# Pooled attention and two feed-forward layers on one core: v in a buffer per head, preparation and weight conversions at other tiles, and layer 1's tanh in two tiles by turns

## The chip, the cores and the metric

One Trainium2 chip, of which one core is used. The metric is the device time of one execution in microseconds (us). Three runs of the kernel before give 1400.29, 1396.39 and 1401.53 us, with 1400.29 us as their median. A separate profiled execution, from which every row below comes, took 1398.61 us.

## What is computed

The reference, cut to what matters (B, H, S, D = 4, 8, 1152, 64):

```python
q_pool = q.reshape(B, H, S // 2, 2, D).mean(axis=3)
scores = (1 / sqrt(D)) * q_pool @ k.transpose(0, 1, 3, 2)
attn = exp(scores - max(scores)); attn = attn / (sum(attn) + 1e-9)
x = (attn @ v) laid out as 2304 tokens x 512
h = x @ w_in;  x = (h - tanh(h)) @ w_out            # layer 1, 512 -> 2048 -> 512
h = x @ w2_in; x = (h * sigmoid(1.702 h)) @ w2_out  # layer 2
```

The weights arrive as 64-bit floats, the rest as 32-bit floats.

## The kernel before

Everything is matrix products of float32 numbers split in a high and a low part, so that one product becomes three matmuls (high x high, high x low, low x high). The order of all instructions on every engine is written out by hand; each engine takes its own in order.

**Attention.** Heads are handled in 16 pairs. A pair has 18 steps (`NS`), nine key tiles of 128 for each of its two heads; the step within the pair is `i`, and the running step is `g`. In a step, `scores(g)` makes a tile of scores on TensorE (PE) in two halves and ScalarE (ACT) takes each half twice through the exponential (`pf` in float32, `ph` rounded); `rest(g-1)` subtracts the two on VectorE (DVE), or on GpSimd (POOL) at i = 2, 5, 8 and 11 of the tile's own step; `pv(g-3)` multiplies with v on PE. At every second step `max_tile` makes a block of scores for the *next* pair and DVE reduces it to row maxima (L284), in one PSUM tile, so the next block waits until the reduction of the last one is done.

The preparation of later pairs lies between: SyncE's queue (SP) loads q, k and v; `prep_qs`, `prep_qh`, `prep_ql`, `prep_kh`, `prep_kl`, `prep_bdq` split them; `stack` copies parts into the layout of the score matmuls (six SP transfers a head); `prep_v(p, s)` splits v of head s of pair p on POOL (L301 and L304). The table `plan` says at which step of a pair each is issued, for the pair two or three ahead. The buffer of v holds a whole pair and there is one: `load_v(p+2)` is issued at i = 14, after `prep_v(p+1, 1)` at i = 12, and `prep_v(p+2, 0)` wants it at i = 3 of the pair that follows.

**Weights of the first steps of layer 1.** The table `when` gives for each of eight pieces of weights (kind `i` for w_in, `o` for w_out) the pair and the step, counted from the end, of its load and of three conversion steps: s0 (one ACT, two DVE instructions, L122 to L127), s1 (two DVE, L134 and L138), and the split (one ACT, L145, one POOL, L146). There are two buffers for raw pieces. What has no step in the table (`ahead`) is done in the first steps of layer 1. `split_x` splits the first block of layer 1's input, one ACT and one POOL instruction for each of four columns.

**Layers.** Each layer is 48 steps `n` (four quarters of the 2048 columns, six blocks of 384 tokens, two halves). A step has 24 matmuls `h_part(n)` and 24 (layer 1) or 18 longer ones (layer 2) `y_part(n-2)` on PE, and `gate(n)` between them. In layer 1 the gate is a polynomial for small h and h - tanh(h) for others: ACT makes u = h*h (L586), d = tanh(h) (L587), later three more squares or cuts of u (L599, L601, L605); DVE makes five instructions (L588, L594, L603, L606, L608), the last of which copies d into g where |h| is large. Between them stand `split_g(n-1)` (ACT L562, POOL L564), which `y_part(n-1)` needs, the additions of y into x (`add`, on ACT in the first quarter, on DVE later) and the conversions of further weights. The tiles u, a, e and d are single, g is double, and h lies in two PSUM tiles.

Of the kernel before, what the change touches and what calls it, by code (L numbers as in the profile page):

```python
# [7 lines left out]
F32 = mybir.dt.float32  # L8
F32R = mybir.dt.float32r
I32 = mybir.dt.int32  # L10
AF = mybir.ActivationFunctionType
ALU = mybir.AluOpType
# [11 lines left out]
def f32(ap):  # L24
    return ap.bitcast(F32)
# [3 lines left out]
def tile_pooled_attention_two_moe(  # L29
# [11 lines left out]
    nc = tc.nc  # L41
    B, NPB, _, S = k.shape
    NT, DM = out.shape
    D = 64
    SP = S // 2
    HB = SP // 2
    KT = S // 128
    QJ = SP // 64
    NPAIR = B * NPB
    TB = 384  # L50
# [10 lines left out]
    wpool = ctx.enter_context(tc.tile_pool(name="wpool", bufs=1))  # L61
# [18 lines left out]
    def new(name, shape, dt=F32R):  # L80
        return wpool.tile(shape, dt, name=name)
# [6 lines left out]
    bdqs = [new(f"bdq{i}", [128, QJ, 128]) for i in range(2)]  # L88
# [9 lines left out]
    def split_x(b, cs, eng):  # L98
        for c in cs:
            hi, lo = xs[b][0][c], xs[b][1][c]  # L100
            nc.scalar.activation(hi, xb[b][:, c], AF.Copy)
            eng.tensor_tensor(lo, xb[b][:, c], f32(hi), op=ALU.subtract)
# [83 lines left out]
    def attention(ctx: ExitStack):  # L186
        ap = ctx.enter_context(tc.tile_pool(name="attn", bufs=1))
# [11 lines left out]
        def fill(i):  # L199
            vh, vl = vt[i]  # L200
            nc.gpsimd.memset(f32(stacks[i][1][D:D + 1, :]), 1.0)
            nc.gpsimd.memset(f32(vh[:, :, D:128]), 1.0)
            nc.gpsimd.memset(f32(vl[:, :, D:128]), 0.0)
# [7 lines left out]
        qraw, kraw, vraw, pairs = {}, {}, {}, {}  # L211
# [5 lines left out]
        def load_k(p):  # L217
            kraw[p] = ap.tile([128, S], F32, tag="kr", name="kr", bufs=2)
            nc.sync.dma_start(out=kraw[p], in_=k[p // NPB, p % NPB])

        def load_v(p):
            vraw[p] = ap.tile([128, 2, KT, D], F32, tag="vr", name="vr")
            nc.sync.dma_start(out=vraw[p], in_=v[p // NPB, p % NPB])

        def prep_qs(p, eng=None):
            pairs[p] = dict(
# [9 lines left out]
        def prep_qh(p):  # L236
            nc.scalar.activation(pairs[p]["qh"], pairs[p]["qs"], AF.Copy)
# [2 lines left out]
            d = pairs[p]  # L240
            nc.vector.tensor_sub(d["ql"], d["qs"], f32(d["qh"][:]))

        def prep_bdq(p):
            qs = pairs[p]["qs"]
            for s in range(2):
                r = slice(64 * s, 64 * s + 64)
                nc.scalar.activation(
                    bdqs[p % 2][r, :, r], qs[r, :].rearrange("p (j c) -> p j c", j=QJ), AF.Copy)

        def prep_kh(p, x):  # L250
            xs = slice(x * SP, (x + 1) * SP)
            nc.scalar.activation(pairs[p]["kh"][:, xs], kraw[p][:, xs], AF.Copy)
# [7 lines left out]
        def prep_kl(p, x):  # L260
            xs = slice(x * SP, (x + 1) * SP)
            nc.gpsimd.tensor_tensor(
                pairs[p]["kl"][:, xs], kraw[p][:, xs], f32(pairs[p]["kh"][:, xs]),
                op=ALU.subtract)
# [12 lines left out]
        def max_tile(p, j, pool=None):  # L277
            d = pairs[p]
            mx = (pool or ps_mx).tile([128, 3, 512], F32, tag="mx", name="mx")
            for a in range(3):  # L280
                nc.tensor.matmul(  # L281
                    mx[:, a, 0:384], bdqs[p % 2][:, j, :], d["kh"][:, a * 384:(a + 1) * 384],
                    start=True, stop=True)
            nc.vector.tensor_reduce(  # L284
                d["mt"][:, j:j + 1], mx[:, :, 0:384], AX.XY, ALU.max, negate=True)
# [10 lines left out]
                    queues[a].dma_start(out=row[:, :, a, :], in_=f32(tt[g:g + QJ, :]))  # L296

        def prep_v(p, s):
            vr = vraw[p]
            vh, vl = vt[(2 * p + s) % 3]  # L300
            nc.gpsimd.tensor_scalar(  # L301
                out=vh[:, :, 0:D], in0=vr[:, s], scalar1=1.0, scalar2=1.0,
                op0=ALU.mult, op1=ALU.mult)
            nc.gpsimd.tensor_tensor(  # L304
                vl[:, :, 0:D], vr[:, s], f32(vh[:, :, 0:D]), op=ALU.subtract)

        probs, accs, halves = {}, {}, {}

# [72 lines left out]

        def spread(p):
            d = norm[p]
            d["rb"] = wpool.tile([128, SP], F32, tag="rb", name="rb", bufs=1)
            for s in range(2):
                r = slice(64 * s, 64 * s + 64)
                row = d["rd"][r, :].rearrange("p i -> (p i)").unsqueeze(0)
                nc.sync.dma_start(out=d["rb"][r, :], in_=row.to_broadcast([64, SP]))

        def normalise(p):  # L390
            ua, rb = norm[p]["ua"], norm[p]["rb"]
# [12 lines left out]
        pool_cast = range(NPAIR * NS - NS + 2, NPAIR * NS, 3)  # L404
        early = {}
        when = (
# [8 lines left out]
        )  # L415
        ahead = []
        for kind, f, *steps in when:
# [3 lines left out]
            ahead += jobs[len(steps):]  # L421
        for c in range(NKC):
            early.setdefault((NPAIR - 1, 13 + c), []).append(
                lambda c=c: split_x(0, [c], nc.gpsimd))

        load_q(0)
        load_k(0)
# [6 lines left out]
            out=pairs[0]["kh"][:, SP:S], in0=kraw[0][:, SP:S],  # L434
            scalar1=1.0, scalar2=1.0, op0=ALU.mult, op1=ALU.mult)
        prep_qh(0)
        prep_ql(0)
        load_q(1)
        load_k(1)
        load_v(0)  # L440
        prep_kl(0, 0)
        prep_kl(0, 1)
        stack(0, 0)
# [3 lines left out]
        with tc.tile_pool(name="ps_first", bufs=2, space=PSUM) as ps_first:  # L447
            for j in range(QJ):
                max_tile(0, j, ps_first)
                if j == 4:  # L450
                    prep_qh(1)
                    prep_kh(1, 0)
                    prep_kh(1, 1)
                    prep_bdq(1)
                    fill(2)
        max_rows(0, (nc.sync, nc.scalar))
        stack(0, 1)
# [2 lines left out]
        prep_v(0, 1)  # L460
        prep_kl(1, 0)
        prep_kl(1, 1)
        load_v(1)
        load_k(2)
        ps_sc = ctx.enter_context(tc.tile_pool(name="ps_sc", bufs=3, space=PSUM))
        ps_mx = ctx.enter_context(tc.tile_pool(name="ps_mx", bufs=1, space=PSUM))
# [4 lines left out]
        for n in range(1, NPAIR):  # L471
# [1 line left out]
                at = (n - 1) * NS - 5 + 2 * j if n > 1 else j + (j + 1) // 2  # L473
                max_at[at] = max_at.get(at, ()) + ((n, j),)
        plan = {
            (2, 2): [(prep_qh,)], (2, 4): [(prep_kh, 0)], (2, 7): [(prep_kh, 1)],
            (2, 10): [(prep_bdq,)], (2, 14): [(prep_ql,), (load_v,)],
            (2, 16): [(prep_kl, 0)], (2, 17): [(prep_kl, 1)], (3, 5): [(load_q,)],
            (3, 7): [(load_k,)], (3, 16): [(prep_qs,)],
        }  # L480
        for g in range(total + LAG):
            p, i = divmod(g, NS)
            n = p + 1
# [43 lines left out]
    def moe(ctx: ExitStack, ending):  # L527
# [4 lines left out]
        for b in range(1, NB):  # L532
            t = mp.tile([128, 2, NKC, TB], F32R, name=f"hl{b}")
# [6 lines left out]
        def temp(nm, bufs=1):  # L540
            return mp.tile([128, 2, TB], F32, tag=nm, name=nm, bufs=bufs)
# [30 lines left out]
        def run(w, place):  # L572
            for go in later.pop((w, place), ()):
                go()

        def gate(n, h, adds):

            g = temp("gg", 2)

            def add(scalar=False):  # L580
                if adds and adds[0][0] is scalar:
                    adds.pop(0)[1]()

            if steps[n][0] == 0:
                u, a, e, d = temp("u"), temp("a"), temp("e"), temp("d")
                nc.scalar.activation(u, h, AF.Square)  # L586
                nc.scalar.activation(d, h, AF.Tanh)  # L587
                nc.vector.scalar_tensor_tensor(  # L588
                    out=g, in0=u, scalar=GC, in1=h, op0=ALU.mult, op1=ALU.mult)
                if n > 0:  # L590
                    split_g(n - 1)
                run(n, "split")
                add()
                nc.vector.tensor_sub(d, h, d)  # L594
                add()
                add()
                add()
                run(n, "convert")
                nc.scalar.activation(a, u, AF.Square, bias=GA0)  # L599
                add(True)  # L600
                nc.scalar.activation(e, u, AF.Square, bias=GB0)  # L601
                add(True)
                nc.vector.scalar_tensor_tensor(  # L603
                    out=g, in0=a, scalar=GA1, in1=g, op0=ALU.add, op1=ALU.mult)
                nc.scalar.activation(a, u, AF.Relu, bias=-T2)  # L605
                nc.vector.scalar_tensor_tensor(  # L606
                    out=g, in0=e, scalar=GB1, in1=g, op0=ALU.add, op1=ALU.mult)
                nc.vector.copy_predicated(g, a[:].bitcast(I32), d)  # L608
            else:
                split_g(n - 1)  # L610
                s = temp("a")
                nc.scalar.activation(s, h, AF.Sigmoid, scale=1.702)  # L612
                run(n, "split")
                add()
                nc.vector.tensor_mul(g, h, s)  # L615
                run(n, "convert")
            gg[n] = g
            while adds:
                adds.pop(0)[1]()
# [73 lines left out]
    with tc.manual_schedule():  # L693
        with ExitStack() as c1:
            ending = attention(c1)
        with ExitStack() as c2:
            moe(c2, ending)
# [44 lines left out]
```

## Time and profile before

| | |
|---|---|
| median of three runs | 1400.29 us |
| profiled execution | 1398.61 us |
| its span, first to last instruction | 1396.8 us |
| PE / DVE / ACT / POOL busy | 1316.1 / 1048.5 / 843.7 / 439.5 us |
| first matmul of layer 1 | 556.17 us |
| chain that ended last | PE 47%, DVE 28%, ACT 9%, DMA 4% |

Time in the profile counts from the first instruction. "Busy" of PE has modelled ends and says little of how near PE is to its peak. The page has a chain of waits that ended last, a table of instruction groups, and a granted TensorE clock for any stretch (1.00 is 2.4 GHz; the other level, 0.50, is 1.2 GHz; a mean between them says how the stretch was shared). Shares are means over stages, and the stages differ: attention up to about 556 us, layer 1 up to about 1001 us, layer 2 after that.

### The profile page before, as it was taken

The page shows a single profiled execution, that of the slowest core. Times are in us where ns is not written, and L with a number is a line of the kernel's source. Part 1 is how long each engine was busy: PE and PEld are TensorE (multiplying, and loading weights), DVE is VectorE, ACT ScalarE, POOL GpSimd, SP SyncE. Part 2 cuts the span into 40 slices and gives each one's busy share as a digit, 9 for nine tenths or more (in the row PEclk, how much of TensorE's full clock was granted, in tenths as well). Part 3 has the DMA queues.
Part 4 walks back from the last instruction along what each step waited for, and adds up shares of the span by engine and source line. Part 5 has one row for each costly group of instructions (what it writes and reads, how often), then busy time and mean ns, then how long its engine had stood idle before and what let it go on. Part 6 is the DMA issues. An engine that isn't in the chain of part 4 may idle for free.

```text
span 1396.8 us, 20802 instructions
## 1 busy us (share of the span) xinstructions
PE 1316.1 (94%) x7632; PEld 1243.2 (89%) x7632; DVE 1048.5 (75%) x1230; ACT 843.7 (60%) x1885; POOL 439.5 (31%) x314
## 2 busy tenths in 40 slices
PE   4999999999999988899999999999999999999998
PEld 3999889998989887899899889899999999999997
DVE  5888887889898878898888888889963554645433
ACT  2798878988888776677656555656643422222211
POOL 6254444444445456233322332332310110110000
PEclk9899999999999999999999999999999999999999
DMA  7466666565667452111110110111110110110011
GB/s 191 123 173 165 154 146 164 148 162 141 165 149 174 102 122 83 58 46 31 46 46 31 42 35 31 46 46 31 46 60 31 46 46 31 52 39 31 24 46 68
DMA packets 44037, 117.70 MB, mean 84 GB/s; under 512 B 11936, under 2 KB 11936, under 8 KB 43936
## 3 DMA queue, kind: packets, MB, share of 16 engines
q1 hardware_dynamic: 43900, 116.38, 31.4%
q8 instruction: 60, 0.98, 0.3%
q14 instruction: 41, 0.34, 0.1%
q10 hardware_dynamic: 36, 0.00, 0.0%
HBM read 66.58 MB, written 4.79 MB: 51 GB/s over the span
## 4 chain that ended last, share of the span: by engine, by line
PE 47%; DVE 28%; ACT 9%; issue 5%; DMA 4%; POOL 3%; SPq 3%; DVEq 0%; POOLq 0%; ACTq 0%
PE y L639 14%; PE h L552 14%; PE pv L348 9%; PE mx L281 4%; DVE gg L606 3%; DVE gg L603 3%; PE sc L319 3%; DVE gg L608 3%; PE sc L320 3%; DVE d L594 3%; DMA vr<-in_v_dram 2%; ACT d L587 2%; DVE wt L123 2%; DVE wt L127 2%; DVE gg L588 2%
## 5 line engine op out<-in xcount | busy, mean ns | idle before, releaser
L321 ACT ACTIVATE pf<-sc 128x288 f32<-128x288 f32 x576 | 243.7, 425 | 75.8 <-PE sc L320 71.9
L323 ACT ACTIVATE ph<-sc 128x288 fp32r<-128x288 f32 x564 | 242.2, 429 | 0.0
L284 DVE TENSOR_REDUCE mt<-mx 128x1 fp32r<-128x1152 f32 x144 | 194.1, 1350 | 57.7 <-PE mx L281 57.4
L332 DVE TENSOR_TENSOR pl<-pf,ph 128x576 fp32r<-128x576 f32 x224 | 208.6, 953 | 6.9 <-ACT ph L323 6.0
L564 POOL TENSOR_TENSOR g<-gg,g 128x768 fp32r<-128x768 f32 x48 | 89.0, 1853 | 300.3 <-ACT g L562 281.0
L319 PE MATMUL sc<-q,a 128*128 128x288 f32 x576 | 169.2, 305 | 9.3 <-ACT pf L321 3.7
L320 PE MATMUL sc<-q,a 65*128 65x288 f32 x576 | 167.3, 303 | 2.6 <-DMA q<-tt 2.6
L612 ACT ACTIVATE a<-h 128x768 f32<-128x768 f32 x48 | 39.0, 812 | 214.5 <-PE h L552 214.5
L348 PE MATMUL pv<-pl,vh 128*128 128x288 f32 x576 | 140.3, 307 | 15.0 <-POOL pl L332 12.2
L652 DVE TENSOR_TENSOR xb<-xb,y 128x384 f32<-128x384 f32 (+1 forms) x126 | 73.0, 606 | 93.2 <-PE y L639 93.2
L348 PE MATMUL pv<-ph,vh 128*128 128x288 f32 x576 | 136.7, 301 | 3.9 <-ACT u L354 3.8
L348 PE MATMUL pv<-ph,vl 128*128 128x288 f32 x576 | 134.5, 297 | 0.0
L281 PE MATMUL mx<-kh,bdq 128*128 128x384 f32 x432 | 108.4, 362 | 24.4 <-DVE mt L284 16.8
L552 PE MATMUL h<-hl,w 128*128 128x384 f32 x720 | 130.5, 335 | 0.0
L332 POOL TENSOR_TENSOR pl<-pf,ph 128x576 fp32r<-128x576 f32 x64 | 107.3, 1676 | 65.3 <-ACT ph L323 55.3
L552 PEld LDWEIGHTS h<-hl,w 128*128 128x128 f32 x720 | 126.4, 188 | 1.2
L319 PEld LDWEIGHTS sc<-q,a 128*128 128x128 f32 x576 | 112.7, 196 | 16.2 <-ACT ph L323 9.9
L605 ACT ACTIVATE a<-u 128x768 f32<-128x768 f32 x48 | 40.7, 848 | 131.8 <-DVE gg L603 131.8
L348 PEld LDWEIGHTS pv<-pl,vh 128*128 128x128 f32 x576 | 96.6, 192 | 20.8 <-POOL pl L332 15.3
L320 PEld LDWEIGHTS sc<-q,a 65*128 65x128 f32 x576 | 111.6, 194 | 3.1 <-issue 3.1
L615 DVE TENSOR_TENSOR gg<-h,a 128x768 f32<-128x768 f32 x48 | 45.8, 955 | 84.8 <-ACT a L612 84.8
L348 PEld LDWEIGHTS pv<-ph,vh 128*128 128x128 f32 x576 | 102.5, 192 | 7.1 <-ACT u L354 6.9
(114 smaller groups left out, 2954.4 us busy)
## 6 DMA issues: line engine op xcount, KB each, us to landing
a<-kh SPq DMA_DIRECT2D x64, 288.0 KB
raw<-in_moe_w_in_dram SPq DMA_DIRECT2D x32, 512.0 KB
raw<-in_moe_w_out_dram SPq DMA_DIRECT2D x32, 512.0 KB
qr<-in_q_dram SPq DMA_DIRECT2D x16, 576.0 KB
kr<-in_k_dram SPq DMA_DIRECT2D x16, 576.0 KB
vr<-in_v_dram SPq DMA_DIRECT2D x16, 576.0 KB
q<-qh SPq DMA_DIRECT2D x64, 144.0 KB
a<-kl SPq DMA_DIRECT2D x32, 288.0 KB
```

The lines of the kernel that those rows point to most:

```text
L281: nc.tensor.matmul(mx[:, a, 0:384], bdqs[p % 2][:, j, :], d["kh"][:, a * 384:(a + 1) * 384], start=True, stop=True)
L284: nc.vector.tensor_reduce(d["mt"][:, j:j + 1], mx[:, :, 0:384], AX.XY, ALU.max, negate=True)
L319: nc.tensor.matmul(sc, a1[:, ks], q2[:, xs], start=True, stop=False)
L320: nc.tensor.matmul(sc, a2[:, ks], q3[:, xs], start=False, stop=True)
L321: nc.scalar.activation(pf[:, xs], sc, AF.Exp, scale=SCALE)
L323: nc.scalar.activation(ph[:, xs], sc, AF.Exp, scale=SCALE)
L332: eng.tensor_tensor(pl, pf, f32(ph[:]), op=ALU.subtract)
L348: nc.tensor.matmul(accs[hd][x], w[:, t, :], r[:, x * HB:(x + 1) * HB], start=(t == 0 and n == 0), stop=(t == KT - 1 and n == 2))
L552: nc.tensor.matmul(hb[:, j, 0:TB], wi[:, c, w, :], x[r][c], start=(k == 0), stop=(k == 3 * NKC - 1))
L564: eng.tensor_tensor(gt[:, :, 1, :], g, f32(gt[:, :, 0, :]), op=ALU.subtract)
L639: nc.tensor.matmul(ys[m][:, 0:w], lhsT, rhs, start=(fp == 0 and k == 0), stop=(fp == 1 and k == 5))
L652: nc.vector.tensor_add(dst, dst, ys[m][:, 0:w])
```

## The change

- v gets a buffer per head (`vr0`, `vr1`); `load_v(p, s)` loads one head. The load for s = 0 is issued at i = 6, the one for s = 1 at i = 14.
- `prep_bdq` is split in its two instructions, at i = 4 and 5 (both at 10 before); `prep_kh` moves from 4 and 7 to 6 and 8; `prep_ql` from 14 to 15. `prep_qs` stays at 16.
- `when` gives other steps to the pieces: conversions of the first three are spread over more steps, the second to last pair takes two whole pieces, the last pair three, and nothing is left for layer 1.
- Two of the four subtractions of the first `split_x` go from POOL to DVE.
- In layer 1, tanh is written into the tile `d` at even n and, from n = 5 on, into the space of the tile `rb` (made larger for it) at odd n.
- One more `add(True)` stands between the ACT instruction L601 and the DVE instruction L603.

```diff
-        def load_v(p):
-            vraw[p] = ap.tile([128, 2, KT, D], F32, tag="vr", name="vr")
-            nc.sync.dma_start(out=vraw[p], in_=v[p // NPB, p % NPB])
+        def load_v(p, s):
+            vraw[p, s] = ap.tile([128, KT, D], F32, tag=f"vr{s}", name=f"vr{s}")
+            nc.sync.dma_start(out=vraw[p, s], in_=v[p // NPB, p % NPB][:, s])
...
         when = (
-            ("i", 0, (-8, 6), (-7, 5), (-7, 8), (-7, 16)),
-            ("i", 1, (-6, 6), (-5, 5), (-5, 8), (-5, 16)),
-            ("o", 0, (-4, 6), (-3, 5), (-3, 8), (-3, 16)),
-            ("i", 2, (-2, 2), (-2, 8), (-2, 11), (-2, 16)),
-            ("i", 3, (-2, 14), (-1, 4), (-1, 5), (-1, 7)),
-            ("o", 1, (-1, 0), (-1, 7), (-1, 8), (-1, 10)),
-            ("o", 2, (-1, 6), (-1, 11), (-1, 12), (-1, 14)),
-            ("o", 3, (-1, 9)),
+            ("i", 0, (-8, 6), (-7, 6), (-7, 14), (-6, 7)),
+            ("i", 1, (-6, 6), (-5, 6), (-5, 14), (-4, 7)),
+            ("o", 0, (-4, 6), (-3, 6), (-3, 14), (-2, 5)),
+            ("i", 2, (-2, 0), (-2, 6), (-2, 12), (-2, 14)),
+            ("i", 3, (-2, 4), (-2, 13), (-2, 15), (-2, 17)),
+            ("o", 1, (-2, 14), (-1, 1), (-1, 3), (-1, 5)),
+            ("o", 2, (-2, 16), (-1, 4), (-1, 6), (-1, 9)),
+            ("o", 3, (-1, 4), (-1, 8), (-1, 10), (-1, 12)),
         )
...
-                lambda c=c: split_x(0, [c], nc.gpsimd))
+                lambda c=c: split_x(0, [c], nc.gpsimd if c < 2 else nc.vector))
...
         plan = {
-            (2, 2): [(prep_qh,)], (2, 4): [(prep_kh, 0)], (2, 7): [(prep_kh, 1)],
-            (2, 10): [(prep_bdq,)], (2, 14): [(prep_ql,), (load_v,)],
+            (2, 2): [(prep_qh,)], (2, 4): [(prep_bdq, 0)], (2, 5): [(prep_bdq, 1)],
+            (2, 6): [(prep_kh, 0), (load_v, 0)], (2, 8): [(prep_kh, 1)],
+            (2, 14): [(load_v, 1)], (2, 15): [(prep_ql,)],
             (2, 16): [(prep_kl, 0)], (2, 17): [(prep_kl, 1)], (3, 5): [(load_q,)],
             (3, 7): [(load_k,)], (3, 16): [(prep_qs,)],
         }
...
-                u, a, e, d = temp("u"), temp("a"), temp("e"), temp("d")
+                u, a, e = temp("u"), temp("a"), temp("e")
+                if n > 4 and n % 2:
+                    d = wpool.tile([128, 2 * TB], F32, tag="rb", name="d2", bufs=1)
+                    d = d.rearrange("p (j t) -> p j t", j=2)
+                else:
+                    d = temp("d")
...
                 nc.scalar.activation(e, u, AF.Square, bias=GB0)
+                add(True)
                 add(True)
```

## Rows read from the trace of the kernel before

**Rows 1.** Stretches: length, engines' busy us (instructions), granted clock, DMA share, GB/s.

```profile
91.00:121.00 30.00, 29.19 (x204) 28.26 (x204) 25.91 (x28) 26.89 (x81) 14.40 (x11) 1.00 0.67 164
443.00:479.00 36.00, 33.02 (x212) 32.07 (x211) 32.01 (x34) 28.09 (x85) 14.74 (x11) 0.91 0.49 104
514.00:556.00 42.00, 34.58 (x225) 31.69 (x225) 32.78 (x34) 29.88 (x89) 24.44 (x19) 0.96 0.36 94
556.00:1001.00 445.00, 424.30 (x2354) 411.82 (x2353) 388.98 (x475) 282.97 (x416) 137.84 (x80) 0.98 0.13 40
1001.00:1396.00 395.00, 390.98 (x1971) 354.68 (x1969) 193.54 (x265) 118.12 (x172) 33.52 (x26) 1.00 0.14 45
```

**Rows 2.** Groups of DVE instructions in layer 1: busy, mean ns, idle before, releaser.

```profile
L588 DVE SCALAR_TENSOR_TENSOR gg<-u,h 128x768 f32<-128x768 f32 x48 | 45.8, 954 | 35.2 <-ACT d L587 33.8 <-issue 1.0
```

**Rows 3.** Instructions in order of time (start, length), end of one gate of layer 1.

```profile
901.59 0.85 ACT L605 ACTIVATE a<-u 128x768 f32<-128x768 f32 x1 [4.06 <-DVE gg L603]
901.66 0.96 DVE L606 SCALAR_TENSOR_TENSOR gg<-e,gg 128x768 f32<-128x768 f32 x1
902.47 0.81 ACT L586 ACTIVATE u<-h 128x768 f32<-128x768 f32 x1
902.73 1.09 DVE L608 COPY_PREDICATED gg<-a,d 128x768 f32<-128x768 int32 x1
903.85 0.81 ACT L587 ACTIVATE d<-h 128x768 f32<-128x768 f32 x1 [0.56 <-DVE gg L608]
...
904.75 0.95 DVE L588 SCALAR_TENSOR_TENSOR gg<-u,h 128x768 f32<-128x768 f32 x1 [0.94 <-ACT d L587]
```

**Rows 4.** The same view, ACT at step n = 1 of layer 1.

```profile
568.97 0.79 ACT L586 ACTIVATE u<-h 128x768 f32<-128x768 f32 x1
569.66 0.80 ACT L587 ACTIVATE d<-h 128x768 f32<-128x768 f32 x1
```

**Rows 5.** The same view, PE, two successive steps of layer 1 without a gap.

```profile
579.55 4.32 PE L552 MATMUL h<-hl,bdq 128*128 128x384 f32 x24
...
587.87 4.32 PE L552 MATMUL h<-hl,w 128*128 128x384 f32 x24
```

**Rows 6.** The same view, attention, POOL and PE after late loads of v.

```profile
138.19 1.04 POOL L301 TENSOR_SCALAR vh<-vr 128x576 fp32r<-128x576 f32 x1 [2.81 <-DMA vr<-in_v_dram]
...
142.76 0.53 PE L348 MATMUL pv<-pl,vh 128*128 128x288 f32 x2 [1.51 <-POOL pl L332]
...
465.99 0.85 PE L348 MATMUL pv<-pl,vh 128*128 128x288 f32 x2 [2.79 <-POOL pl L332]
```

**Rows 7.** The same view, attention, PE in pairs that convert weights.

```profile
334.92 0.79 PE L281 MATMUL mx<-kh,bdq 128*128 128x384 f32 x3 [1.16 <-DVE mt L284]
...
405.68 0.80 PE L281 MATMUL mx<-kh,bdq 128*128 128x384 f32 x3 [1.99 <-DVE mt L284]
...
495.07 0.53 PE L348 MATMUL pv<-pl,vh 128*128 128x288 f32 x2 [1.53 <-POOL pl L332]
```

**Rows 8.** The same view, start of the last pair: scores on PE, SP, ACT.

```profile
519.71 0.29 PE L319 MATMUL sc<-q,a 128*128 128x288 f32 x1
...
521.04 0.29 PE L319 MATMUL sc<-q,a 128*128 128x288 f32 x1
...
522.49 1.31 SPq L109 DMA_DIRECT2D raw<-in_moe_w_in_dram  x1
...
528.29 0.67 ACT L122 ACTIVATE wa<-raw 128x512 f32<-128x512 f32 x1 [2.81 <-DMA raw<-in_moe_w_in_dram]
```

**Rows 9.** The same view, DVE at step n = 0 of layer 1.

```profile
563.82 0.41 DVE L123 TENSOR_SCALAR wt<-raw 128x512 int32<-128x512 int32 x1
...
566.40 0.95 DVE L603 SCALAR_TENSOR_TENSOR gg<-a,gg 128x768 f32<-128x768 f32 x1
```

**Rows 10.** The same view, DVE at i = 14 and 16 of a pair.

```profile
346.87 0.75 DVE L241 TENSOR_TENSOR ql<-qs,qh 128x576 fp32r<-128x576 f32 x1
...
350.14 0.75 DVE L234 TENSOR_TENSOR qs<-qr 128x576 f32<-128x576 f32 x1
```

More of the change, by code (lines that the diff above doesn't have):

```diff
@@ L241, in prep_ql, with prep_bdq @@
             nc.vector.tensor_sub(d["ql"], d["qs"], f32(d["qh"][:]))
[L243 to L248, printed above, removed]
+        def prep_bdq(p, s):
+            r = slice(64 * s, 64 * s + 64)
+            nc.scalar.activation(
+                bdqs[p % 2][r, :, r],
+                pairs[p]["qs"][r, :].rearrange("p (j c) -> p j c", j=QJ), AF.Copy)
         def prep_kh(p, x):
@@ L298, in prep_v @@
         def prep_v(p, s):
-            vr = vraw[p]
+            vr = vraw.pop((p, s))
             vh, vl = vt[(2 * p + s) % 3]
             nc.gpsimd.tensor_scalar(
-                out=vh[:, :, 0:D], in0=vr[:, s], scalar1=1.0, scalar2=1.0,
+                out=vh[:, :, 0:D], in0=vr, scalar1=1.0, scalar2=1.0,
                 op0=ALU.mult, op1=ALU.mult)
             nc.gpsimd.tensor_tensor(
-                vl[:, :, 0:D], vr[:, s], f32(vh[:, :, 0:D]), op=ALU.subtract)
+                vl[:, :, 0:D], vr, f32(vh[:, :, 0:D]), op=ALU.subtract)
         probs, accs, halves = {}, {}, {}
@@ L383, in spread @@
             d = norm[p]
-            d["rb"] = wpool.tile([128, SP], F32, tag="rb", name="rb", bufs=1)
+            d["rb"] = wpool.tile([128, 2 * TB], F32, tag="rb", name="rb", bufs=1)
             for s in range(2):
@@ L387, in spread @@
                 row = d["rd"][r, :].rearrange("p i -> (p i)").unsqueeze(0)
-                nc.sync.dma_start(out=d["rb"][r, :], in_=row.to_broadcast([64, SP]))
+                nc.sync.dma_start(out=d["rb"][r, 0:SP], in_=row.to_broadcast([64, SP]))
         def normalise(p):
@@ L439, in attention @@
         load_k(1)
-        load_v(0)
+        load_v(0, 0)
+        load_v(0, 1)
         prep_kl(0, 0)
@@ L453, in attention @@
                     prep_kh(1, 1)
-                    prep_bdq(1)
+                    prep_bdq(1, 0)
+                    prep_bdq(1, 1)
                     fill(2)
@@ L462, in attention @@
         prep_kl(1, 1)
-        load_v(1)
+        load_v(1, 0)
+        load_v(1, 1)
         load_k(2)
```

## The prediction

> **What bounds the kernel now.** I read the granted clock and the busy time by stretch first [rows 1]. Layer 2 is the plain stage: PE is busy 390.98 of 395 us there and nothing in the change touches it, so I count it as it is. Layer 1 takes 445 us. A step of it, h and y together, needs 587.87 - 579.55 = 8.32 us of PE when nothing is late [rows 5], so its 48 steps need 399 us, and some 46 us are lost. DVE is busy for 389 us of the same 445, which is nearly as much work as PE has, so any gap on DVE is a candidate. The group table for DVE then names one gap: before L588, the first DVE instruction of a gate, it stood idle for 35.2 us, of which 33.8 ended with the tanh [rows 2]; these are 34 of the 48 gates.
>
> The instructions in order of time show how that gap comes about [rows 3]. ACT has u(n) done by 903.3, but its tanh L587 begins at 903.85, right behind the end of L608 (902.73 + 1.09 = 903.82), the last reader of the single tile d. L588 begins at 904.75, 0.09 behind the tanh. So in these gates DVE ends a gate, waits for one whole tanh and goes on: 0.94 us each. That is the first thing that the change takes away.
>
> Attention takes the first 556 us. There I looked for pairs that are slower than their like: the stretch from 91 to 121 holds about a pair (204 matmuls in 30 us), the one from 443 to 479 also (212), in 36 us at a granted clock of 0.91 [rows 1]. The PE instructions with the longest waits fall in two kinds. In four pairs POOL's split of v began late because its load had not landed (2.81 us in the one shown), POOL's next subtraction was then late for PE, and PE stood 1.51 to 2.79 us [rows 6]. In pairs that convert weights, four row-maximum blocks waited 1.16 to 1.99 us for DVE, and three value products some 1.5 us for a POOL that had a weight's split in its queue [rows 7].
>
> **The change part by part.**
>
> **Tanh in two tiles.** From n = 5 on, tanh(n) has no reader of an earlier d before it but that of n - 2, long done. It can follow u(n) at once. At n = 1, where nothing held it, the tanh began 0.69 us after u [rows 4]. In the gate shown u began at 902.47, so the tanh would run from 903.16 to 903.97 and L588 start 0.09 later, at 904.06 in place of 904.75: 0.69 us [rows 3]. If L588 needed only u, it could start with the end of L608, and 904.75 - 903.82 = 0.93 would be won. I take the first, since L588 follows the tanh by 0.09 though it doesn't read d [rows 3]: 34 x 0.69 = 23.5 us [rows 2]; upper bound 34 x 0.93 = 31.6. Where a POOL instruction stretches L606, ACT is already through and the whole 0.93 is won, so I put 25. The lower bound is what is left if PE then becomes the limit or the new order of ACT delays L599: half, 12 us.
>
> The Trainium skill, page "PSUM — Partial Sum Buffer", section "PSUM bank collisions raise a hardware error", says that two engines that read one PSUM bank in the same place at one time collide, and that software therefore orders them. By it L588 (reads h) has to stay behind the tanh (reads h) after the change too, and the sum would be the 23.5; without it, the 31.6. The 0.09 in the row agrees with the rule.
>
> **Nothing of the weights left for layer 1.** At n = 0, DVE does four conversion instructions between L594 and L603, from 563.82 to 566.40 [rows 9]: 2.6 us on the way to the first g, for which PE waits then. They and a POOL split go: 3 us, from 2 to 4. The rest of layer 1's start is as before. DVE's 389 us less nothing, with some 12 us of idle left, against PE's 399: the two nearly meet, so I take 1 off for stalls that then show at PE. Layer 1: 25 + 3 - 1 = 27 us, bounds 14 and 34. The extra `add(True)` puts one ACT copy ahead of L605, which waited 4.06 us for DVE in the gate shown [rows 3]: nothing; without that cover, one copy in six gates.
>
> **v in two buffers.** The first half's load goes out at i = 6, some 15 steps ahead of its use, in place of 7. The four PE waits go, 1.51 and 2.79 being the first and last and 8.0 us their sum [rows 6], and some of the clock lost in the pair at 0.91 (36 x 0.09 = 3.2 us [rows 1]), because that pair holds the longest of them. I take 10, bounds 6 and 12. There are 32 issues in place of 16 on SP. At i = 6 SP now waits for POOL's split of the v before it; behind it stand `load_k` and the copies of the pair's ends, none of which is wanted for several steps. If POOL is late there, the cost is on `load_k`, wanted a pair later: nothing.
>
> **Weight conversions elsewhere.** The waits of rows 7 sum to about 9.8 us over four such blocks and three such products. s0 goes from i = 5 to 6 and stands between the same two reductions on DVE as before, so its share stays; s1 goes from 8 to 14 where POOL is idle; the split from 16 to 7, away from the kl subtractions. I take half, 5 us; bounds 1 and 8.
>
> **`prep_ql` one step later.** It now stands with `prep_qs` between the same two reductions: 0.75 + 0.75 us [rows 10] where each had a stretch of its own. A delay of at most 0.75 us in 13 pairs, mostly taken up in the next stretch: I take 0.1 us a pair, 1 in all; bounds 0 and 10. `prep_bdq` and `prep_kh` are the same ACT work, in single steps rather than two together: nothing, bounds -3 and +3. Two subtractions of `split_x` leave POOL for DVE where POOL is the later one: a gain of about 1, counted below. Attention to the last pair: 10 + 5 - 1 = 14, bounds 4 and 20.
>
> **The last pair is where the change costs.** Before, the load of piece i3 is issued at (-2, 14), lands at 528.29 and ACT, which wants it at (-1, 4), waits 2.81 us [rows 8]. SP gets to it only at 522.49, because the ten transfers of i = 13 stand before it. The change puts the load of o1 at the same place, but wants it at (-1, 1), three steps sooner. A step there takes 521.04 - 519.71 = 1.33 us [rows 8], so the wait of ACT grows from 2.81 to 2.81 + 4.0 = 6.8 us, and `scores`, `rest` and PE stand behind it in order. The cost is 4.0; bounds 2 and 8, the upper one if the clock falls after so long a gap, as it did around 466 [rows 1, 6]. Against it stand fewer lumps late in the pair (the stretch to 556 is busy on PE for only 34.58 of 42 us [rows 1]) and the lighter POOL: I give back 2, bounds 0 and 5. Last pair: 2 lost, bounds 8 lost and 3 won.
>
> **The sum.** 27 + 14 - 2 = 39 us off the profiled execution: 1398.6 - 39 = 1359.6. The median of the runs lies 1.7 above that execution, within their spread of 5; I forecast 1360 us. The ends of all terms together give 14 + 4 - 8 = 10 and 34 + 20 + 3 = 57, so 1389 and 1342 us.
>
> **The rivals.** (a) PE or ACT takes the place of the tanh: PE has 399 us of work and DVE 389, so as DVE's gaps close, y waits for g and h for its PSUM tile. For it: the two are 10 us apart. Against it: the gaps lie in stretches where DVE is behind, not PE. Layer 1 then gains 14 in place of 27: 1373 us. (b) The last pair swallows what attention gains: 8 lost at its start with a fallen clock and 5 won before, so 27 + 5 - 8 = 24: 1376 us. (c) The two tiles don't do what they should, because taking the space of `rb` again brings a wait for L608 of the step before. Then L588's 33.8 us stay, and 3 + 14 - 2 = 15 are left: 1385 us. Nothing in the trace speaks for it. (d) Slower: `prep_ql` and `prep_qs` in one stretch make the row-maximum block of every pair late, each pair shows a PE gap, and the clock falls after it. The stretch around 466 is 6 us longer than the one at 91 [rows 1], which is the most that such a gap with its clock has cost. In 13 pairs it decides from 39 / 13 = 3 us a pair on; at 4 a pair the sum is 52 - 39 = 13 lost: 1412 us. Against it: a delay of 0.75 us can hardly make a gap of 3.
>
> **How the numbers follow.** The forecast 0.6, its own range 1347 to 1374; (a) 0.13; (b) 0.12; (c) 0.06; (d) 0.04; 0.05 for what I don't see, a little on the side of no change. A measurement of this kernel can tell about 0.5%, or 7 us, from no change. Forecast, (a), (b) and most of (c) are faster by more than that: 0.90; same 0.05; slower 0.05. The range takes in (a), (b), most of (c) and the low bound: 1342 to 1385.
>
> **What the profile will show.** Right: DVE's idle time before L588 falls from 35 to under 13 us; L587 begins 0.7 us after L586; no PE wait of over 1 us behind POOL's split of v; the first y of layer 1 comes 3 us sooner after the first h; an ACT wait of 5 to 7 us for raw weights early in the last pair. Wrong, if L587 still begins with the end of L608, if the steps of layer 1 stay near 9 us, or if pairs of attention without conversions take over 31 us.

## The result

The changed kernel takes 1352.6 us (median; 1352.1 to 1353.1), against 1398.3 for the kernel before in the same measurement: a ratio of 0.968, with a 95% interval of 0.964 to 0.971. A second measurement gave 1352.4 against 1397.7 us, 0.969 (0.967 to 0.971). The forecast was 1360 us, with 1342 to 1385 as its range; about 45 us were gained where 39 were forecast. One further execution of the changed kernel, the one profiled first, was disturbed from start to end, took 3239 us and is left out, so all rows below for the changed kernel are of the second measurement (span 1350.7 us).

The stretches of the changed kernel (length, then busy us of PE, of its weight loads (`PEld` in the profile), of DVE, ACT and POOL with instructions, granted clock, DMA share, GB/s), which answer to [rows 1]:

```profile
89.00:120.00 31.00, 29.85 (x210) 28.92 (x209) 28.50 (x30) 27.37 (x83) 15.28 (x11) 1.00 0.64 159
427.00:458.00 31.00, 29.89 (x207) 28.65 (x206) 29.20 (x32) 27.46 (x83) 15.23 (x11) 1.00 0.53 121
491.00:536.00 45.00, 35.01 (x225) 32.45 (x224) 37.11 (x42) 30.12 (x89) 23.50 (x18) 0.92 0.29 76
536.00:955.00 419.00, 412.13 (x2355) 407.17 (x2355) 387.36 (x472) 279.54 (x414) 136.03 (x79) 1.00 0.13 42
955.00:1350.00 395.00, 390.84 (x1970) 354.53 (x1968) 193.25 (x265) 117.98 (x172) 33.53 (x26) 1.00 0.14 45
```

Layer 1 falls from 445 to 419 us, 26 us, with the same DVE work (389 and 387 us). Layer 2 is unchanged at 395. Attention ends 20 us sooner: the first matmul of layer 1 is at 536.21 in place of 556.17. Within attention, the last transposes of row maxima (one per pair on DVE, so a clock of the pairs) come at 491.34 in place of 513.61, 22.3 us sooner, and from there to layer 1 the changed kernel is 2.3 us *slower*, at a clock of 0.92 where the kernel before had 0.96 [rows 1].

The DVE group that answers to [rows 2] (busy, mean ns, idle before, releaser):

```profile
L596 DVE SCALAR_TENSOR_TENSOR gg<-u,h 128x768 f32<-128x768 f32 x48 | 45.7, 953 | 11.0 <-ACT d L595 10.6
```

And the end of one gate, instructions in order of time, answering to [rows 3]:

```profile
699.62 0.81 ACT L594 ACTIVATE u<-h 128x768 f32<-128x768 f32 x1
699.87 1.09 DVE L617 COPY_PREDICATED gg<-a,d 128x768 f32<-128x768 int32 x1
700.33 0.80 ACT L595 ACTIVATE d<-h 128x768 f32<-128x768 f32 x1
701.06 0.85 ACT L565 ACTIVATE g<-gg 128x768 fp32r<-128x768 f32 x1
701.22 0.95 DVE L596 SCALAR_TENSOR_TENSOR gg<-u,h 128x768 f32<-128x768 f32 x1 [0.26 <-ACT d L595]
```

The tanh (L595) now begins 0.71 us after u, while the copy that ends the last gate (L617) is still running. DVE's first multiply still waits for the end of the tanh, but for 0.26 us in place of 0.94.

### The profile page after: what moved, and what is told of

Same layout as the page of the kernel before. It is cut to its first block, busy times and chain, and to the rows that moved or that the text cites. A ratio compares the mean times of both kernels' runs of the same rounds, so it can differ in the third digit from the quotient of the medians.

```text
span 3236.7 us, 20882 instructions
## 1 busy us (share of the span) xinstructions
PE 3217.4 (99%) x7632; PEld 2620.4 (81%) x7632; DVE 1003.4 (31%) x1232; ACT 870.4 (27%) x1885; POOL 409.4 (13%) x312
## 3 DMA queue, kind: packets, MB, share of 16 engines
q1 hardware_dynamic: 46204, 116.38, 13.4%
## 4 chain that ended last, share of the span: by engine, by line
PE 99%; DVE 0%; DMA 0%; SPq 0%; issue 0%; ACT 0%; DVEq 0%
PE h L555 32%; PE y L648 32%; PE pv L347 18%; PE sc L319 6%; PE sc L318 6%; PE mx L280 6%; DMA qr<-in_q_dram 0%; DVE mt L283 0%; DVE qs L234 0%; SPq L295 0%; DVE bdq L257 0%; SPq L273 0%; DVE ql L241 0%; SPq L271 0%; SPq L274 0%
## 5 line engine op out<-in xcount | busy, mean ns | idle before, releaser
L320 ACT ACTIVATE pf<-sc 128x288 f32<-128x288 f32 x576 | 236.8, 411 | 627.3 <-PE sc L319 624.6
L319 PE MATMUL sc<-q,a 65*128 65x288 f32 x576 | 327.5, 569 | 2.1 <-DMA q<-tt 2.1
L555 PE MATMUL h<-hl,w 128*128 128x384 f32 x720 | 328.2, 681 | 0.0
L318 PE MATMUL sc<-q,a 128*128 128x288 f32 x576 | 325.6, 565 | 1.4 <-DVE mt L283 1.4
L347 PE MATMUL pv<-ph,vh 128*128 128x288 f32 x576 | 274.7, 567 | 0.0
L555 PE MATMUL h<-hl,bdq 128*128 128x384 f32 x600 | 274.0, 680 | 0.0
L347 PE MATMUL pv<-pl,vh 128*128 128x288 f32 x576 | 273.8, 568 | 0.0
L347 PE MATMUL pv<-ph,vl 128*128 128x288 f32 x576 | 273.7, 568 | 0.0
L555 PEld LDWEIGHTS h<-hl,bdq 128*128 128x128 f32 x600 | 208.5, 349 | 62.0 <-issue 60.2
L322 ACT ACTIVATE ph<-sc 128x288 fp32r<-128x288 f32 x564 | 230.2, 408 | 0.0
L648 PE MATMUL y<-w,g 128*128 128x512 f32 x324 | 217.8, 828 | 0.0
L347 PEld LDWEIGHTS pv<-ph,vl 128*128 128x128 f32 x576 | 202.2, 364 | 4.9 <-issue 2.2
```

What stands on the lines that cost most here:

```text
L318: nc.tensor.matmul(sc, a1[:, ks], q2[:, xs], start=True, stop=False)
L319: nc.tensor.matmul(sc, a2[:, ks], q3[:, xs], start=False, stop=True)
L320: nc.scalar.activation(pf[:, xs], sc, AF.Exp, scale=SCALE)
L322: nc.scalar.activation(ph[:, xs], sc, AF.Exp, scale=SCALE)
L347: nc.tensor.matmul(accs[hd][x], w[:, t, :], r[:, x * HB:(x + 1) * HB], start=(t == 0 and n == 0), stop=(t == KT - 1 and n == 2))
L555: nc.tensor.matmul(hb[:, j, 0:TB], wi[:, c, w, :], x[r][c], start=(k == 0), stop=(k == 3 * NKC - 1))
```

## Experiments

### The tanh alone

Put back in the changed kernel:

```diff
-                u, a, e = temp("u"), temp("a"), temp("e")
-                if n > 4 and n % 2:
-                    d = wpool.tile([128, 2 * TB], F32, tag="rb", name="d2", bufs=1)
...
+                u, a, e, d = temp("u"), temp("a"), temp("e"), temp("d")
```

> The changed kernel with one tile d for tanh again; all else as changed. Theory: the wait of the tanh for the end of the gate before comes back in some 34 gates at 0.69 to 0.93 us, so 24 to 31 us slower than the changed kernel, 1376 to 1384 us, with attention as in the changed kernel. Rival (PE has become the limit of layer 1, so DVE's gaps are covered): less than 12 us slower.

Measured: 1375.3 us, 23.0 more than the changed kernel, 1 us under what was expected. DVE's idle time before the multiply is back at the 35.2 us of the kernel before:

```profile
L591 DVE SCALAR_TENSOR_TENSOR gg<-u,h 128x768 f32<-128x768 f32 x48 | 45.8, 954 | 35.2 <-ACT d L590 33.8 <-issue 1.0
```

The same edit alone, in the kernel before (the first lines of that diff the other way round, and the larger `rb`):

> The kernel before with the tanh in two tiles by turns and nothing else changed. Theory: 23 to 30 us faster than before, 1368 to 1376 us, all of it in layer 1, and attention is as before. Rival (the two tiles help only because layer 1 also starts with less to do): less than 12 us faster.

Measured: 1374.6 us against 1397.7, 23.1 less, and 11.9 us of idle time before the multiply. The two medians give the same price, to 0.1 us, which is closer than executions of one kernel agree (1373.7 to 1376.1 us in the first of these runs). So the tanh's part stands by itself, needs nothing of the rest, and is half of the whole gain. The rival that PE would cover it falls.

### Why 0.27 us are left: the two reads of h

```diff
                 nc.scalar.activation(u, h, AF.Square)
-                nc.scalar.activation(d, h, AF.Tanh)
                 nc.vector.scalar_tensor_tensor(
                     out=g, in0=u, scalar=GC, in1=h, op0=ALU.mult, op1=ALU.mult)
+                nc.scalar.activation(d, h, AF.Tanh)
```

> The changed kernel with the multiply g = GC u h on DVE written ahead of the tanh on ACT, both of which read h. Theory (the two reads of h are kept apart, whichever comes first): now the tanh waits for the multiply, and h - tanh(h) starts about 1.9 us after the end of the gate before in place of 1.1, so about 0.75 us more in some 40 gates, 20 to 32 us slower than the changed kernel. Rival (they may overlap, and the 0.27 us that DVE still waits is only the tanh's lateness): 0 to 8 us faster.

Measured: 1419.8 us, 67 more than the changed kernel, and slower than the kernel before. One gate in order of time:

```profile
901.48 0.81 ACT L594 ACTIVATE u<-h 128x768 f32<-128x768 f32 x1
901.74 1.09 DVE L617 COPY_PREDICATED gg<-a,d 128x768 f32<-128x768 int32 x1
902.77 0.95 DVE L595 SCALAR_TENSOR_TENSOR gg<-u,h 128x768 f32<-128x768 f32 x1
...
903.75 0.81 ACT L597 ACTIVATE d<-h 128x768 f32<-128x768 f32 x1 [1.46 <-DVE gg L595]
...
904.60 0.96 DVE L602 TENSOR_TENSOR d<-h,d 128x768 f32<-128x768 f32 x1 [0.41 <-ACT d L597]
```

Now it is the tanh that waits, and it begins 0.03 us after the multiply ends (902.77 + 0.95 = 903.72). So the two reads of h exclude each other whichever is written first, as this program is ordered, and in this gate the tanh is the one to write first. The loss is more than twice what I expected. DVE's rows for layer 1 say where 62 of the 67 us lie, first in the changed kernel, then in this one:

```profile
L123 DVE TENSOR_SCALAR wt<-raw 128x512 int32<-128x512 int32 x31 | 33.0, 1063 | 0.0
```

```profile
L123 DVE TENSOR_SCALAR wt<-raw 128x512 int32<-128x512 int32 x31 | 54.2, 1748 | 0.0
L602 DVE TENSOR_TENSOR d<-h,d 128x768 f32<-128x768 f32 x48 | 46.0, 958 | 34.3 <-ACT d L597 34.3
```

DVE's idle time before the multiply and before h - tanh(h) (L602) goes from 11.0 to 36.5 us, 25.5 more, which is what I expected. The other 37 us are its busy time, 387 us in the changed kernel and 424 here, and I had not counted them. More than half of them are L123, the first DVE instruction of a conversion, which takes 1.75 us on average in place of 1.06. It took 0.42 us the one time that POOL was idle, and twenty times 2.00 us or more here, each time right behind the start of POOL's split of g (L567), as in this one:

```profile
876.11 1.86 POOL L567 TENSOR_TENSOR g<-gg,g 128x768 fp32r<-128x768 f32 x1 [5.55 <-ACT g L565]
876.20 2.04 DVE L123 TENSOR_SCALAR wt<-raw 128x512 int32<-128x512 int32 x1
```

The longest in the changed kernel was 1.56 us. Behind the late tanh stands ACT's copy of the g before (L565, at 904.46), which POOL's split waits for. That this delay is what moved the split onto L123 is argued from the order of the rows, and was not tried alone.

The Trainium skill, page "PSUM — Partial Sum Buffer", section "PSUM bank collisions raise a hardware error", says that software must keep two engines off one PSUM bank at the same time. Both runs agree with it, with 0.09 us between the two reads in one order and 0.03 in the other; they show the order and not the reason for it.

### The load of o1 in the last pair

The first expectation below is for the changed kernel itself, whose rows stand above and here; the second is for this edit.

```diff
-            ("o", 1, (-2, 14), (-1, 1), (-1, 3), (-1, 5)),
+            ("o", 1, (-2, 12), (-1, 1), (-1, 3), (-1, 5)),
```

> The changed kernel itself, for an undisturbed trace. Theory, from the sum: 1353 us again; DVE's idle time before the first instruction of a gate falls from 35 us to 8 to 13 us (34 gates keep 0.25 us each); the tanh begins 0.7 us after u; layer 1 takes 416 to 420 us in place of 445, attention ends 10 to 18 us sooner, and early in the last pair ACT waits 5 to 7 us for raw weights. Rival (the gain is all in attention): layer 1 stays above 435 us and attention ends 40 us sooner.

> The changed kernel with the load of the piece o1 issued at (-2, 12) in place of (-2, 14), so that it stands ahead of the ten transfers of i = 13 on SP. Theory of the prediction's last-pair step: the wait of ACT for these weights at (-1, 1), forecast at 6.8 us, goes, and the kernel gains 3 to 7 us on the changed one. Rival (the wait is covered, or the ten transfers come late by as much in its place): within 2 us of the changed kernel.

The changed kernel kept to the first, but for attention, which ended 20 us sooner where 10 to 18 were expected. In it, SP, ACT and PE, in order of time:

```profile
491.57 3.14 SPq L295 DMA_DIRECT2D q<-tt  x4
...
498.91 0.74 SPq L274 DMA_DIRECT2D q<-ql  x1
499.76 1.26 SPq L109 DMA_DIRECT2D raw<-in_moe_w_out_dram  x1
...
504.93 0.68 ACT L122 ACTIVATE wa<-raw 128x512 f32<-128x512 f32 x1 [5.47 <-DMA raw<-in_moe_w_out_dram]
...
505.96 0.61 PE L318 MATMUL sc<-q,a 128*128 128x288 f32 x1 [5.34 <-ACT pf L320]
```

Ten transfers hold SP from 491.57 to 499.65, the load goes out behind them and lands for ACT at 504.93, after 5.47 us of waiting, and PE stood for 5.34. At the end of that wait the granted clock was at 0.50, its lower level, and stayed there for 6.8 us in all; in the run with the earlier load it is 1.00 over the whole stretch (views of the changed kernel and of that run):

```profile
504.60:511.40 6.80, 5.44 (x22) 5.35 (x23) 6.33 (x9) 5.08 (x15) 2.79 (x2) 0.50 0.24 74
```

```profile
491.00:530.00 39.00, 31.99 (x217) 29.26 (x216) 36.60 (x42) 29.21 (x88) 24.06 (x18) 1.00 0.34 88
```

With the load two steps earlier, ahead of the ten:

```profile
490.55 0.33 SPq L109 DMA_DIRECT2D raw<-in_moe_w_out_dram  x1
491.31 0.80 SPq L295 DMA_DIRECT2D q<-tt  x1
...
498.87 0.78 ACT L122 ACTIVATE wa<-raw 128x512 f32<-128x512 f32 x1
...
504.90 0.66 ACT L122 ACTIVATE wa<-raw 128x512 f32<-128x512 f32 x1 [1.61 <-DMA raw<-in_moe_w_out_dram]
```

ACT doesn't wait at all for o1 (498.87); 1.61 us come back with the next piece, o2. Measured: 1347.2 us, 5.1 less than the changed kernel, ratio to before 0.965 (0.963 to 0.968). The step of the last pair is shown, and a better kernel with it.

### Where attention gained more than forecast

Up to the last pair 14 us were forecast, 20 at most, and 22.3 came. From the second transposes to the last, first in the kernel before and then in the changed one:

```profile
60.24:513.61 453.37, 424.99 (x2898) 409.50 (x2897) 393.40 (x419) 384.13 (x1137) 213.19 (x157) 0.98 0.62 151
465.50:472.30 6.80, 6.31 (x25) 6.31 (x26) 5.68 (x6) 2.90 (x9) 2.06 (x3) 0.50 0.22 66
```

```profile
59.55:491.34 431.79, 417.49 (x2904) 404.02 (x2903) 399.08 (x419) 383.91 (x1140) 222.92 (x157) 1.00 0.64 160
```

The stretch is 21.6 us shorter. PE's idle time in it fell by 14.1 us and its busy time, for the same matmuls, by 7.5: the granted clock was 0.98 before and is 1.00. In the kernel before it stood at 0.50 for 13.6 us, in three pieces, of which the longest is shown; this one and another came with waits of PE of 2.79 and 2.14 us for POOL's late subtraction. At half the clock 13.6 us do the work of 6.8, so a third of the gain goes with the clock, for which the prediction had 2 us.

Three runs undo one part each. v in one buffer again, loaded whole at i = 14:

```diff
-            vraw[p, s] = ap.tile([128, KT, D], F32, tag=f"vr{s}", name=f"vr{s}")
+            vraw[p] = ap.tile([128, 2, KT, D], F32, tag="vr", name="vr")
...
-            (2, 6): [(prep_kh, 0), (load_v, 0)], (2, 8): [(prep_kh, 1)],
-            (2, 14): [(load_v, 1)], (2, 15): [(prep_ql,)],
+            (2, 6): [(prep_kh, 0)], (2, 8): [(prep_kh, 1)],
+            (2, 14): [(load_v,)], (2, 15): [(prep_ql,)],
```

> The changed kernel with one buffer for both heads' v again, loaded whole at i = 14; all else as changed. Attention gained 22 us up to the last pair where 14 were forecast (10 for v, 5 for the conversions, less 1). Theory A (late v delays POOL in ordinary pairs too, so v is worth more than its four large waits): 13 to 18 us slower than the changed kernel's 1352.4. Forecast term as it stands: 6 to 12 us slower. Theory B (the 8 us came from the other moves): no more than 10 slower.

Measured: 1355.0 us, 2.7 more than the changed kernel. That is within theory B alone, and 7 us from the term, which put 10 on v. The size is rough: this kernel's executions lie between 1353.3 and 1359.4 us.

The old table `when` (the diff stands ahead of the prediction, the other way round):

> The changed kernel with the old table of weight conversions; all else as changed. By the forecast the new table is worth 5 us in attention and 3 at the start of layer 1, and costs 2 to 4 in the last pair: 4 to 7 us slower than the changed kernel, with the first y of layer 1 some 3 us later after the first h. Theory B (the conversions were worth more): over 9 us slower.

Measured: 1356.5 us (1354.0 to 1358.1), 4.2 more, as forecast. The first y of layer 1 comes 15.1 us after the first h, as in the kernel before; in the changed kernel 12.5.

The old steps of `prep_bdq`, `prep_kh` and `prep_ql`:

```diff
-            (2, 2): [(prep_qh,)], (2, 4): [(prep_bdq, 0)], (2, 5): [(prep_bdq, 1)],
-            (2, 6): [(prep_kh, 0), (load_v, 0)], (2, 8): [(prep_kh, 1)],
-            (2, 14): [(load_v, 1)], (2, 15): [(prep_ql,)],
+            (2, 2): [(prep_qh,)], (2, 4): [(prep_kh, 0)], (2, 6): [(load_v, 0)],
+            (2, 7): [(prep_kh, 1)], (2, 10): [(prep_bdq, 0), (prep_bdq, 1)],
+            (2, 14): [(prep_ql,), (load_v, 1)],
```

> The changed kernel with prep_bdq, prep_kh and prep_ql at their old steps (10; 4 and 7; 14), v still in two buffers. The forecast put 0 (-3 to +3) on bdq and kh and a loss of 1 on ql: 1351 to 1353 us. Theory B (spreading ACT's preparation is where the 8 us of attention beyond the forecast came from): 5 to 9 us slower than the changed kernel.

Measured: 1362.5 us, 10.1 more, about one us in each pair, just beyond the 5 to 9 of theory B. So theory B holds in kind: what I had put at nothing is the largest part of attention's gain. Which of the three moves it is, the next run asks; only `prep_bdq` goes back:

```diff
-            (2, 2): [(prep_qh,)], (2, 4): [(prep_bdq, 0)], (2, 5): [(prep_bdq, 1)],
+            (2, 2): [(prep_qh,)], (2, 10): [(prep_bdq, 0), (prep_bdq, 1)],
```

> The changed kernel with only prep_bdq back at i = 10, both instructions together. With bdq, kh and ql all at their old steps the changed kernel lost 10 us, where the forecast had put nothing on bdq and kh. Theory: it is bdq, because at i = 10 it stands on ACT right ahead of the copy of the sums out of PSUM, for which PE waits (about 0.4 us in each pair, 13 such waits in the trace with the old steps, none in the changed kernel's), and behind which the exponentials come late: 7 to 11 us slower than the changed kernel. Rival (it is ql, which no longer shares a stretch of DVE with qs, or kh): less than 3 us slower.

Measured: 1365.8 us, 13.4 more, beyond the 7 to 11 that were expected. ACT and PE of this kernel, in order of time:

```profile
241.06 1.38 ACT L245 ACTIVATE bdq<-qs 64x576 fp32r<-64x576 f32 x2
...
243.63 0.75 ACT L353 ACTIVATE u<-pv 128x288 f32<-128x288 f32 x2
...
244.12 0.40 PE L347 MATMUL pv<-ph,vh 128*128 128x288 f32 x1 [0.38 <-ACT u L353]
```

And its waits between 60 and 490 us (in total, times, longest; PEld is PE's weight loads):

```profile
PEld sc L318 <- ACT ph L322: 8.2, 22, 0.4
PEld pv L347 <- ACT u L353: 7.7, 13, 0.6
PE pv L347 <- ACT u L353: 4.7, 13, 0.4
PE sc L318 <- ACT ph L322: 2.1, 11, 0.2
```

The two `prep_bdq` instructions stand on ACT ahead of four exponentials of a tile of scores (L320, L322) and, behind these, the copy that empties the sums of one head (L353). The copy is not right behind them, as was expected, but nothing between makes up for their 1.38 us: the first value product of the next head waits for the copy, 13 waits, once a pair, and scores wait for L322. Of these four rows the changed kernel has one left:

```profile
PEld sc L318 <- ACT ph L322: 1.5, 7, 0.2
```

The weight loads' two waits are thus 15.9 us in place of 1.5, 14.4 more, which is about the whole price of 13.4. PE's own records show less of it, 6.8 us (4.7 + 2.1), and their ends are modelled. Why bdq alone costs 3 us more than with kh and ql at their old steps is open.

The same waits stand in the trace of the kernel before (60 to 513 us), where the prediction could have found them:

```profile
PEld pv L348 <- ACT u L354: 6.4, 11, 0.6
PE pv L348 <- ACT u L354: 3.8, 10, 0.4
```

Each is 0.6 us at most, and the prediction went by the longest waits.

### What v in two buffers was worth

In the changed kernel PE waits for a row maximum 23 times between 60 and 490 us, 0.9 us at most and 11.5 in all. DVE and POOL before one of them, and PE:

```profile
101.82 1.34 DVE L283 TENSOR_REDUCE mt<-mx 128x1 fp32r<-128x1152 f32 x1
103.09 0.74 DVE L331 TENSOR_TENSOR pl<-pf,ph 128x576 fp32r<-128x576 f32 x1
103.76 2.52 DVE L396 TENSOR_TENSOR xb<-u,rb 128x384 f32<-128x384 f32 x2
106.19 1.34 DVE L283 TENSOR_REDUCE mt<-mx 128x1 fp32r<-128x1152 f32 x1
...
103.15 1.21 POOL L300 TENSOR_SCALAR vh<-vr 128x576 fp32r<-128x576 f32 x1
104.44 1.61 POOL L303 TENSOR_TENSOR vl<-vr,vh 128x576 fp32r<-128x576 f32 x1
...
107.59 0.62 PE L280 MATMUL mx<-kh,bdq 128*128 128x384 f32 x2 [0.92 <-DVE mt L283]
```

L396 is `normalise`, two multiplies at i = 4. POOL's split of v (L300, L303), no longer late, now runs beside them. Two runs put `normalise` at i = 10, in the changed kernel and in the one with a single v buffer:

```diff
-            if p > 1 and i == 4:
+            if p > 1 and i == 10:
                 normalise(p - 2)
```

> The changed kernel with normalise(p - 2), two DVE multiplies, at i = 10 in place of 4. With v on time, POOL's split of v at i = 3 runs beside them and each takes 1.2 to 1.4 us in place of 0.7 to 1.0, and after them PE waits 0.9 us for a row maximum in eight pairs. Theory: at i = 10, where POOL has less to do, the multiplies fall back to under 0.9 us and these waits go: 5 to 9 us faster than the changed kernel, 1343 to 1347 us. Rival (the lump on DVE costs the same wherever it stands): within 2 us.

> The kernel with one buffer for both heads' v (1355.0 us) and normalise at i = 10. Theory (v on time was worth about 8 to 10 us, but gave most of it back through the collision of POOL and DVE at i = 4): without that collision the single buffer's price shows, so this one is 6 to 11 us slower than the kernel with two buffers and normalise at 10. Rival (v on time is worth the 2.7 us that were measured): 1 to 4 us slower than that one.

Measured: 1346.9 us in the changed kernel, 5.4 less; 1353.1 with the single buffer. The multiplies between 60 and 490 us in the changed kernel, then with `normalise` at 10, then with the single buffer and `normalise` at 4:

```profile
L396 DVE TENSOR_TENSOR xb<-u,rb 128x384 f32<-128x384 f32 x13 | 17.8, 1373 | 0.0
L396 DVE TENSOR_TENSOR xb<-u,rb 128x192 f32<-128x192 f32 x13 | 15.9, 1227 | 0.0
```

```profile
L396 DVE TENSOR_TENSOR xb<-u,rb 128x384 f32<-128x384 f32 x13 | 7.1, 549 | 0.0
L396 DVE TENSOR_TENSOR xb<-u,rb 128x192 f32<-128x192 f32 x13 | 7.0, 539 | 0.0
```

```profile
L396 DVE TENSOR_TENSOR xb<-u,rb 128x384 f32<-128x384 f32 x13 | 9.6, 736 | 0.0
L396 DVE TENSOR_TENSOR xb<-u,rb 128x192 f32<-128x192 f32 x13 | 7.4, 572 | 0.0
```

The larger of the two takes 0.55 us at i = 10 and 1.37 on average beside POOL at i = 4. Together they take 33.7 us with v on time and 17.0 with v late: that the collision came with the second buffer is shown. PE's waits turn with it: with two buffers in place of one, those behind POOL's subtraction fall from 6.2 to 1.8 us, and those for a row maximum rise from 7.4 to 11.5. Without the collision the two buffers are worth 1353.1 - 1346.9 = 6.2 us by medians, at the low end of what was expected, and with it 2.7, so by these figures more than half of the gain of v on time was given back to DVE. How much is uncertain: the executions of the single buffer with `normalise` at 10 lie between 1349.5 and 1356.2 us, and by them alone 6.2 can't be told from the 1 to 4 us of the rival.

The Trainium skill, page "SBUF — State Buffer", section "Who interferes with whom", says that a DVE instruction with two inputs in SBUF and a GpSimd instruction that reads SBUF hold a shared port against each other. These multiplies have two such inputs, and the rows agree: 0.55 against 1.37 us for the larger.

### Both improvements together

The changed kernel with the load of o1 at (-2, 12) and `normalise` at i = 10:

> The changed kernel with both: the load of o1 at (-2, 12) and normalise at i = 10. The two lie in different stretches (start of the last pair; step 4 of every pair), so their gains should add: 5 from the first as measured, 5 to 9 from the second, 1338 to 1342 us. Rival (one of them only moves a wait on to the next engine): 1345 us or more.

Measured: 1342.0 us, ratio to before 0.960 (0.959 to 0.962), 10.4 less than the changed kernel, where the two alone gave 5.1 and 5.4. They add.

## Why the prediction was right, point by point

- **Tanh in two tiles.** Right in mechanism and size: 25 us with 23.5 as the count of rows; 23.0 and 23.1 measured. One of the 34 gates counted is the first of the layer, which waits 2.89 us in both kernels and which the change doesn't touch; the other 33 make 33 x 0.69 = 22.8. The idle time fell to 11.0 us (under 13 was forecast), 0.27 a gate where 0.25 were worked out, because the multiply stays behind the tanh. The granted clock of layer 1 rose too, from 0.98 to 1.00, but the 24.2 us by which this idle time fell leave little of the layer's 26 for it.
- **Start of layer 1.** Forecast 3 us; the first y follows the first h after 12.5 us in place of 15.1, 2.6 sooner. Layer 1 as a whole: 27 forecast, 26 measured.
- **The last pair.** The one loss that was forecast is there. The wait of ACT was put at 6.8 us and is 5.47, so it grew by 2.7 and not by 4.0; the net loss was put at 2 and is 2.3, with a lower clock (0.92 where it was 0.96).
- **Conversions.** 4.2 us for the whole table, against the 4 to 7 that the prediction's terms (5, plus 3 in layer 1, less what the last pair loses) make. In that run's trace the last transposes come 5.2 us later than in the changed kernel, where 5 were put on attention. Of the three value products that the prediction calls late by some 1.5 us, one waited 0.62; the sum of 9.8 is right.
- **v in two buffers.** The mechanism is there: up to the last pair no wait of PE behind POOL's subtraction is over 0.4 us, where there were waits of 1.51 to 2.79 [rows 6]. The size was wrong: 10 us, bounds 6 and 12, against 2.7. The step that failed is that I summed four waits of PE, added 2 us of clock, and called them v's. With one buffer and the other moves kept, POOL still waits for v up to 3.1 us, yet PE stands at most 1.72 for it, and of the stretches at the lower clock one of 3.4 us comes back. And I did not ask what POOL, once on time, would run beside.
- **`prep_bdq` and `prep_kh`.** The step that failed most: "the same ACT work, in single steps rather than two together: nothing, bounds -3 and +3". It was worth 10 us with ql, and bdq alone 13.4. I counted ACT's work and not who waits behind it: the exponentials, the copy L353 and, behind them, PE. This miss and the one on v go opposite ways: that attention came out 8 us from its 14, and the whole 6 from its 39, is in part luck. The bounds of 4 and 20 for attention left out the 10 us that `prep_ql` could lose by its own bounds, and the 3 either way of `prep_bdq`; the 22.3 lie outside them.
- **`prep_ql`** (rival d): no pair lost 3 us; pairs without conversions take 29.6 to 30.9 us between transposes, where the kernel before took 30.4 to 34.2 in the same stretch (60 to 300 us). The rivals (a), (b) and (c) fall with the first three points.

The parts undone one by one make 23.0 + 10.1 + 4.2 + 2.7 = 40 us of 45. Where the other 5 lie is not shown: the parts may be worth more together than one by one, and the two subtractions moved off POOL and the extra `add(True)` were not tried alone.

## What to carry to other kernels

When an instruction only moves within its engine's queue, the price is not its own length but the one of whatever stands behind it with another engine waiting: look for copies out of PSUM behind it. Here each such wait was of 0.6 us at most and there was one in each pair, so a list of the longest waits doesn't show them and a list of sums does. A wait that several things end late cannot be priced by summing it under one name; undo the one cause and see what the others leave. And before bringing an engine's work forward in time, look at what its neighbours do at that moment: here a transfer that came on time put POOL's split of v beside two DVE multiplies, which took twice as long for it (33.7 us in place of 17.0).

## What was not expected of the hardware

Two DVE multiplies of 128x384 and 128x192 took 0.55 and 0.54 us on average at i = 10 and 1.37 and 1.23 us beside POOL's split of v. In the kernel before, with POOL late, they fell between. And the order of two engines on one PSUM tile was worth 67 us of 1352, at the price of no instruction.
